# The last pair's second layer as word products instead of products of quarters

## The chip, the cores and the metric

The kernel runs on one core of a Trainium2 chip. The metric is the time of one execution on the device in microseconds (us), the median of several runs. Engines are named as in the profile: PE is TensorE (matrix products, with PEld for its weight loads), DVE is VectorE, ACT is ScalarE, POOL is GpSimd, SP is SyncE, which here only issues transfers. Each engine works through its own instructions strictly in order and waits for others by semaphores.

## The reference

A state-space scan (Mamba-2) over 4 batches, 8 heads and 768 tokens gives a matrix x of 3072 tokens by 256. Then comes a feed-forward block with an ELU between its two layers:

```python
def _moe_ref(x, w_in, w_out):          # x 3072x256, w_in 256x2048, w_out 2048x256
    h = x @ w_in
    alpha = 1.0
    g = np.where(h > 0.0, h, alpha * (np.exp(np.minimum(h, 0.0)) - 1.0))
    return (g @ w_out).astype(np.float32)

x = np.ascontiguousarray(attn_out.transpose(0, 2, 1, 3)).reshape(B * S, H * D)
return _moe_ref(x=x, **moe_kwargs)
```

The change touches `g @ w_out` for the last 512 tokens alone. The weights come to the kernel as 64-bit floats and are turned into float32 in it.

## The kernel before

The 3072 tokens are cut into 12 blocks of 256, numbered 0 to 11 (`n`), and worked on in pairs (n, n + 1). The scan of a later pair is mixed into the feed-forward work of an earlier one. The order of all instructions is written out by hand (a manual schedule): what stands first in the program stands first in the queue of its engine.

**First layer** (`l1_words`, L778, from block 2 on). For each of 16 slices `m` of 128 hidden units it makes h for 512 tokens (two blocks) as three passes over exact 12-bit words. An activation is y1 * 4096 - y0 and a weight is w1 + w0, each word short enough to be exact in TensorE's float32r form; the third pass multiplies sums of words, so that three products do for four. Each pass is two matrix products (L788) of 128x512. The results lie in two PSUM tiles, `ps_h` and `ps_w`. Then:

- ScalarE scales `ps_w` into e (L796), VectorE joins both into `ps_h` (L799);
- `begin_end` (L803): ScalarE's Relu of -h (L805) and Exp (L806) into e;
- `end_words` (L810), called one step later, ahead of the next L799: VectorE's L813 makes g from e and `ps_h` and so frees the PSUM tile. For even m, GpSimd subtracts the first half of g from the second (L817, the helper `sub` of L848), in preparation for the products of quarters.

**Second layer** (`second`, L871). g and w_out of one pair of blocks are taken as 2x2 quarters and multiplied with seven products of quarters instead of eight (Winograd's form). Each of the seven (r = 0 to 6) is made in two halves of the hidden units; one half of one r is four chunks i with two token tiles ts, so eight float32 products of 128x128 (L907), and a pair has 2 x 7 x 8 = 112. The sums of quarters of w_out are made once (`a_out`, `s_out`). The sums of quarters of g are made by GpSimd (`sum_t2`, L863, and the in-place subtractions after r = 0 and r = 1, L922 and L927, all through L848). VectorE and ScalarE add each finished product into `p_sum` and `c_sum` (L885, L919, L944, L959).

**The order.** In the loop of L1310, the first layer of pair n and the second layer of pair n - 2 are interleaved: step k issues `l1_words` for m = k, then some of the scan of a later pair, then `begin_end`, then three or four chunks of `second` (`l2s`). For the last pair (n = 10, where `m` is None) no scan is left; its steps hold only first layer and the second layer of pair 8 (L1330), 56 chunks in all. After it, L1354 runs the second layer of pair 10 by itself. There `last` is set: finished quarters of the output are stored early, and the last product is cut in two (L888 to L899), so that the last store is small.

**PSUM.** Two pools share the eight banks: `ps_a` has seven tiles, which `ps_h`, `ps_w` and every second product of quarters take in turn; `ps_o` has one, which the other products of quarters take.

**SBUF.** Tiles are reused by tag. `w_in` has nine buffers, `w64` eleven, `g0` and `g1` twelve each. At the last pair the `w_in` buffers hold the low words of w_in, and `w64` its high words and the sums of quarters of w_out.

Of the kernel before, what the change touches and what calls it, by code (L numbers as in the profile page):

```python
# [10 lines left out]
F32 = mybir.dt.float32  # L11
U32 = mybir.dt.uint32
BF16 = mybir.dt.bfloat16
F32R = mybir.dt.float32r
ALU = mybir.AluOpType
ACT = mybir.ActivationFunctionType

P = 128
Q = 64
BLK = 2 * P  # L20
CW = 256
WORD = 2.0 ** 12
NEAR = 1.0 + 2.0 ** -13
# [9 lines left out]
def kernel(  # L33
# [27 lines left out]
    nc = tc.nc  # L61
# [3 lines left out]
    NP = NB * NG  # L65
    BH = NB * NH
    ROWS = BH * NG
    DM, DF = moe_w_in.shape
    w_in64, w_out64 = moe_w_in.bitcast(U32), moe_w_out.bitcast(U32)
    KC, MC = DM // P, DF // P  # L70
# [12 lines left out]
    def psum(shape, name):  # L83
        return p_a.tile(shape, F32, tag="a", name=name)
# [7 lines left out]
    for k in range(4):  # L92
        (nc.scalar if k % 2 else nc.sync).dma_start(
            out=la0[BH * k:BH * (k + 1)],
# [715 lines left out]
    def end_words():  # L810
        n, m, h, e = late.pop(0)
        g_of[n, m] = ffn.tile([P, 2, BLK], F32, tag=f"g{m % 2}", name="g", bufs=12)
        nc.vector.scalar_tensor_tensor(  # L813
            out=g_of[n, m].rearrange("p b i -> p (b i)"), in0=e, scalar=1.0, in1=h,
            op0=ALU.subtract, op1=ALU.max)
        if m % 2 == 0 and (n, m) != (2, 14):
            sub(g_of[n, m][:, 1], g_of[n, m][:, 1], g_of[n, m][:, 0])  # L817

    def row_of(n):
        b, g = place(n)  # L820
        return b * S + g * BLK
# [25 lines left out]
    def sub(out, in0, in1):  # L847
        nc.gpsimd.tensor_tensor(out=out, in0=in0, in1=in1, op=ALU.subtract)  # L848

    def quarters(n, i):  # L850


        if n == 2 and i < DIRECT:
            A, B = g_of[n, i], g_of[n + 1, i]
            return A[:, 0], A[:, 1], B[:, 0], B[:, 1]
        A, B = g_of[n, 2 * i], g_of[n, 2 * i + 1]
        return A[:, 0], B[:, 0], A[:, 1], B[:, 1]
# [10 lines left out]

    c_of = {}

    def second(n, last=False):  # L871


        c = c_of[n] = ffn.tile([P, 2, 2, 2, P], F32, tag="c", name="c_sum", bufs=1)
        c11, c12, c21, c22 = (c[:, at, :, e] for e in range(2) for at in range(2))
        a11, a12, s1, a22 = a_out
        s2, s3, s4 = s_out
        for half in range(2):
            if not half:
                tmp = ffn.tile([P, 3, 2, P], F32, tag="tmp", name="p_sum", bufs=1)  # L880
                p1, p5, u = (tmp[:, r] for r in range(3))
            chunk = range(4 * half, 4 * half + 4)

            def add(out, in0, in1, eng=nc.vector):
                eng.tensor_tensor(out=out, in0=in0, in1=in1, op=ALU.add)  # L885

            for r, a in enumerate((a11, a12, s1, s2, s3, a22, s4)):
                if last and half and r == 6:  # L888
                    store(n, 0)
                    for ts, queue in enumerate((nc.scalar, nc.sync)):  # L890
                        ps = psum([P, P], "ps_o")
                        for i in chunk:
                            nc.tensor.matmul(  # L893
                                out=ps, lhsT=quarters(n, i)[3][:, ts * P:(ts + 1) * P],
                                rhs=a[:, i], start=(i == chunk[0]), stop=(i == chunk[-1]))
                        nc.vector.tensor_tensor(
                            out=c12[:, ts], in0=ps, in1=c12[:, ts], op=ALU.add)
                        r0 = row_of(n + 1) + ts * P
                        queue.dma_start(out=out[r0:r0 + P, 0:P], in_=c12[:, ts])  # L899
                    return  # L900
                pool, tag = (p_a, "a") if (7 * half + r) % 2 else (p_o, "o")
                ps = pool.tile([P, 2, P], F32, tag=tag, name="ps_o")
                for i in chunk:
                    b11, b21, b12, b22 = quarters(n, i)
                    b = (b11, b21, b12, t2_of[n, i], b11, b21, b22)[r]
                    for ts in range(2):
                        nc.tensor.matmul(  # L907
                            out=ps[:, ts], lhsT=b[:, ts * P:(ts + 1) * P], rhs=a[:, i],
                            start=(i == chunk[0] and ts == 0), stop=(i == chunk[-1]),
                            skip_group_check=True)  # L910
                    if i < chunk[-1]:
                        yield
                if r == 0:
                    if half:
                        add(p5, ps, c22)
                        add(c21, ps, c21)
                        add(c11, ps, c11)
                    else:
                        nc.scalar.copy(out=p1, in_=ps)  # L919
                    for i in chunk:  # L920
                        b11 = quarters(n, i)[0]
                        sub(b11, t2_of[n, i], b11)  # L922
                elif r == 1:
                    add(c11, ps, c11 if half else p1)
                    for i in chunk:
                        b21 = quarters(n, i)[1]
                        sub(b21, b21, t2_of[n, i])  # L927
                elif r == 2:
                    add(p5, ps, p5 if half else p1)
                elif r == 3:  # L930
                    add(p5, ps, p5)
                    if half:
                        add(c12, c12, p5, nc.gpsimd)
                        add(c21, ps, c21)
                    else:
                        add(u, ps, p1)
                elif r == 4:
                    if half:
                        add(c21, ps, c21)
                    else:  # L940
                        add(u, ps, u)
                    add(c22, ps, p5)
                    if not half:
                        nc.scalar.copy(out=c12, in_=ps)  # L944
                    if last and half:
                        r0 = row_of(n + 1)
                        nc.sync.dma_start(
                            out=out[r0:r0 + BLK, P:2 * P].rearrange("(t p) c -> p t c", p=P),
                            in_=c22)
                    if not half:  # L950
                        sum_t2(n, 1)
                    elif n + 2 < NP:
                        sum_t2(n + 2, 0)
                elif r == 5:
                    add(c21, ps, c21 if half else u)
                elif half:
                    add(c12, ps, c12)
                else:
                    nc.vector.tensor_tensor(out=c12, in0=ps, in1=c12, op=ALU.subtract)  # L959
                yield  # L960

    def store(n, at):
        r0 = row_of(n + at)
        nc.sync.dma_start(
            out=out[r0:r0 + BLK, :].rearrange("(t p) e -> p t e", p=P),
            in_=c_of[n][:, at].rearrange("p t e c -> p t (e c)"))
# [343 lines left out]
    for n in range(4, NP, 2):  # L1310
        m = n + 2 if n + 2 < NP else None
        steps = second(n - 2)

        def l2s(count):
            for _ in range(count):
                next(steps)

        for k in range(16):
            l1_words(n, k, between=m if k == 15 else None)
            turn_step(n, k // 2 * 2 + 1, k % 2)  # L1320
            if n == 4 and k == 0:
                decay(6, 1)
            if m:
                stage_scan(n, k)
            begin_end()
            if k == 0 and n > 4:
                store(n - 4, 0)
                store(n - 4, 1)
            if not m:
                l2s(4 if k % 2 else 3)  # L1330
                continue
            l2s((3 + (n == 4), 3 - (n == 4), 3, 3, 3, 3, 3, 3, 4 + 4 * (n == 4), 5 - 4 * (n == 4),
                 2, 2, 3, 1, 1, 0)[k])
            if k == 9:
                scores(m, m + 1)
                sums(m, m + 1)
                for q in range(4):
                    weigh_two(m, q)
                l2s(2)
                states(m)  # L1340
            if k == 10:
                states(m + 1)
            if k == 13:
                y = across(m, m + 1)
                inside(y, m, m + 1, ts=(0,))
                l2s(4)
                inside(y, m, m + 1, ts=(1,))
        if m:
            l2s(4)
            both_of_y(m)  # L1350
        end_words()
        for _ in steps:
            pass
    n = NP - 2  # L1354
    for k, _ in enumerate(second(n, True)):
        if k == 0:
            store(n - 2, 0)
            store(n - 2, 1)


# [28 lines left out]
```

## Time and profile before

| What | us |
|---|---|
| Median of 3 runs (347.1 to 347.92) | 347.36 |
| The profiled execution, whole | 347.65 |
| Its span in the trace | 345.9 |

Busy time in the span by stretch, us (the first layer of the last pair runs from about 267 to 316, its second layer from 317.65 to 342.7):

| Stretch | PE | DVE | ACT | POOL |
|---|---|---|---|---|
| 0 to 100 | 96.22 | 83.51 | 79.86 | 60.86 |
| 100 to 150 | 49.97 | 41.22 | 41.30 | 45.35 |
| 150 to 210 | 60.00 | 45.00 | 42.73 | 35.77 |
| 210 to 268 | 57.85 | 42.49 | 42.92 | 34.96 |
| 268 to 316 | 48.00 | 31.57 | 28.79 | 23.08 |
| 316 to 346 | 26.67 | 9.48 | 2.47 | 15.23 |

How to read the lines of a profile: a timeline line has the start, the duration, the engine, the line of the program, the operation, the tiles it writes and reads, partitions x elements with the type, and how many instructions were merged into it (x2); in brackets stands how long the engine had been idle before, and what ended that. A line of the chain of work that ended last has the start, the time until the next piece takes over, and the work. Matrix products are pipelined, so a single one is recorded longer than the distance to the next; the distance is what counts. GpSimd's and VectorE's records overlap their neighbours in the same way, by some hundredths of a microsecond. The granted TensorE clock is 0.99 or 1.00 of full speed in each of the stretches above.

### The profile page before, as it was taken

How to read it: one execution, taken by the hardware profiler on the slowest of the kernel's cores; microseconds unless marked ns; L12 is line 12 of the kernel's file. 1: busy time of each engine (PE TensorE's matmuls, PEld its weight loads, DVE VectorE, ACT ScalarE, POOL GpSimd, SP SyncE). 2: the span in 40 equal slices, each digit the busy share in tenths (PEclk: the TensorE clock that was granted, in tenths of full speed). 3: DMA queues.
4: the chain of work that ended last, by engine and by line, in shares of the span. 5: the costliest groups of instructions: out<-in, count | busy, mean ns of one | idle time of the engine just before them, and what ended most of it. 6: DMA issues, size and time to landing. Idle time of an engine off the chain costs nothing.

```text
span 345.9 us, 9861 instructions
## 1 busy us (share of the span) xinstructions
PE 338.7 (98%) x3878; PEld 297.4 (86%) x3878; DVE 253.3 (73%) x504; ACT 238.1 (69%) x541; POOL 215.3 (62%) x321
## 2 busy tenths in 40 slices
PE   8989999999999999999999999999999999999996
PEld 4669888888788898889899888999988999999996
DVE  4898988879898778866788676878676766665222
ACT  5688989599759898657699457699457566565000
POOL 5553553559989699964396664296754264455760
PEclk9999999999999999999999999999999999999999
DMA  8888988470797961070511170410000100001001
GB/s 145 228 231 165 326 178 236 87 140 30 107 151 112 139 108 31 10 162 2 124 45 32 17 153 5 116 22 3 2 0 4 63 0 3 0 0 63 2 1 62
DMA packets 76902, 28.58 MB, mean 83 GB/s; under 512 B 57848, under 2 KB 71736, under 8 KB 76856
## 3 DMA queue, kind: packets, MB, share of 16 engines
q1 hardware_dynamic: 70360, 25.60, 32.2%
q0 software_dynamic: 4176, 2.10, 5.4%
q8 instruction: 30, 0.49, 0.6%
q10 hardware_dynamic: 2320, 0.26, 0.5%
q14 instruction: 16, 0.13, 0.1%
HBM read 22.51 MB, written 3.34 MB: 75 GB/s over the span
## 4 chain that ended last, share of the span: by engine, by line
PE 92%; SPq 2%; DMA 2%; DVE 1%; ACT 1%; issue 1%; POOL 0%; POOLq 0%; ACTq 0%
PE ps_o L907 36%; PE ps_h L788 19%; PE ps_h L671 11%; PE ps_w L788 10%; PE ps_o L832 8%; PE ps_y L638 3%; DMA w<-in_moe_w_in_dram 2%; PE ps_g L545 2%; PE ps_y L620 2%; PE ps_st L575 1%; SPq L179 1%; PE ps_o L893 1%; SPq L132 0%; POOL w_in L252 0%; SPq L116 0%
## 5 line engine op out<-in xcount | busy, mean ns | idle before, releaser
L907 PEld LDWEIGHTS ps_o<-w_out,g 128*128 128x128 f32 x640 | 78.6, 192 | 3.4
L907 PE MATMUL ps_o<-w_out,g 128*128 128x128 f32 x640 | 80.3, 276 | 0.0
L805 ACT ACTIVATE e<-ps_h 128x512 f32<-128x512 f32 x72 | 43.0, 597 | 50.2 <-DVE ps_h L799 50.1
L813 DVE SCALAR_TENSOR_TENSOR g<-e,ps_h 128x512 f32<-128x512 f32 x72 | 49.4, 686 | 34.1 <-ACT e L806 33.7
L848 POOL TENSOR_TENSOR g<-g 128x256 f32<-128x256 f32 x36 | 28.0, 777 | 56.2 <-DVE g L813 56.0
L799 DVE SCALAR_TENSOR_TENSOR ps_h<-ps_h,e 128x512 f32<-128x512 f32 x72 | 50.1, 695 | 12.5 <-ACT e L796 9.7
L788 PE MATMUL ps_w<-y_both,w_words 128*128 128x512 f32 x144 | 51.1, 435 | 0.0
L796 ACT ACTIVATE e<-ps_w 128x512 f32<-128x512 f32 x72 | 42.2, 587 | 12.9 <-PE ps_w L788 12.8
L671 PE MATMUL ps_h<-yT,w_in 128*128 128x256 f32 (+1 forms) x208 | 45.2, 368 | 2.3 <-POOL w_in L252 2.2
L806 ACT ACTIVATE e<-e 128x512 f32<-128x512 f32 x72 | 45.5, 632 | 2.3
L788 PE MATMUL ps_h<-y,w_words 128*128 128x512 f32 x144 | 46.1, 402 | 0.0
L788 PE MATMUL ps_h<-y,w 128*128 128x512 f32 x144 | 44.7, 392 | 0.0
L671 PEld LDWEIGHTS ps_h<-yT,w_in 128*128 128x128 f32 x208 | 36.4, 190 | 8.3 <-POOL w_in L252 3.7
L525 ACT ACTIVATE L<-L,ncum 128x64 f32<-128x64 f32 x160 | 42.2, 336 | 0.2
L907 PE MATMUL ps_o<-w_sum,g 128*128 128x128 f32 x304 | 38.4, 275 | 0.0
L907 PEld LDWEIGHTS ps_o<-w_sum,g 128*128 128x128 f32 x304 | 37.0, 192 | 1.2 <-ACT c_sum L944 0.2
L530 POOL TENSOR_SCALAR_AFFINE_SELECT L<-L 64x512 f32<-64x512 f32 x40 | 30.0, 749 | 9.1 <-ACT L L525 7.7
L788 PEld LDWEIGHTS ps_h<-y,w 128*128 128x128 f32 x144 | 27.1, 188 | 6.5 <-POOL w L848 0.2
L848 POOL TENSOR_TENSOR g<-t,g 128x256 f32<-128x256 f32 x40 | 28.0, 730 | 5.9 <-PE ps_o L907 5.7
L788 PEld LDWEIGHTS ps_h<-y,w_words 128*128 128x128 f32 x144 | 26.4, 188 | 5.7 <-issue 0.4
L832 PE MATMUL ps_o<-w_out,g 128*128 128x256 f32 x128 | 31.0, 384 | 0.0
L848 POOL TENSOR_TENSOR t<-g 128x256 f32<-128x256 f32 x40 | 28.6, 746 | 0.2
(131 smaller groups left out, 535.1 us busy)
## 6 DMA issues: line engine op xcount, KB each, us to landing
L<-flat SPq DMA_DIRECT2D x20, 256.0 KB
w<-in_moe_w_out_dram SPq DMA_DIRECT2D x8, 512.0 KB
w<-in_moe_w_in_dram SPq DMA_DIRECT2D x7, 512.0 KB
xr<-in_x_dram SPq DMA_DIRECT2D x24, 128.0 KB
out_dram<-c_sum SPq DMA_DIRECT2D x9, 256.0 KB
bc<-in_B_dram SPq DMA_DIRECT2D x24, 64.0 KB
w_sum<-w_out POOLq DMA_DIRECT2D x3, 512.0 KB, 8.9
bc<-in_C_dram SPq DMA_DIRECT2D x22, 64.0 KB
```

The source lines that it names most:

```text
L525: nc.scalar.activation(L[:, h, u], L[:, h, u], ACT.Exp, bias=ncum[:, u, row:row + 1])
L530: nc.gpsimd.affine_select(out=part, in_=part, pattern=[[0, 4], [0, 2], [1, Q]], compare_op=ALU.is_ge, fill=0.0, base=0, channel_multiplier=-1)
L671: nc.tensor.matmul(out=ps[:, j, toks], lhsT=w_in[i][:, k, j * P:(j + 1) * P], rhs=yT[n // 2][:, k, n % 2].rearrange("p u i -> p (u i)")[:, ...
L788: nc.tensor.matmul(out=ps, lhsT=lhs[:, k], rhs=rhs[:, k], start=k == 0 and lhs is not w0, stop=k == KC - 1 and lhs is not w1)
L796: nc.scalar.activation(e, both, ACT.Copy, scale=WORD)
L799: nc.vector.scalar_tensor_tensor(out=high, in0=high, scalar=WORD - 1.0, in1=e, op0=ALU.mult, op1=ALU.add)
L805: nc.scalar.activation(e, high, ACT.Relu, scale=-1.0)
L806: nc.scalar.activation(e, e, ACT.Exp, scale=-1.0)
L813: nc.vector.scalar_tensor_tensor(out=g_of[n, m].rearrange("p b i -> p (b i)"), in0=e, scalar=1.0, in1=h, op0=ALU.subtract, op1=ALU.max)
L832: nc.tensor.matmul(out=o_of[n][:, ts], lhsT=g_of[n, j][:, m % 2, ts * P:(ts + 1) * P], rhs=w_out[:, m], start=(m == 0 and ts == 0), stop=( ...
L848: nc.gpsimd.tensor_tensor(out=out, in0=in0, in1=in1, op=ALU.subtract)
L907: nc.tensor.matmul(out=ps[:, ts], lhsT=b[:, ts * P:(ts + 1) * P], rhs=a[:, i], start=(i == chunk[0] and ts == 0), stop=(i == chunk[-1]), s ...
```

## The change

For the last pair, `second` is replaced by `second_words`, and preparations for it are put into the pair's first layer.

- **Words of w_out** (`words_of_out(m)`, 16 calls of one slice each): a scaled high word `v1` on ScalarE, and two instructions on VectorE that make the low word `v0` and the sum `vb`. For even m, GpSimd first puts the slice into a new tile w, half of it copied and half as the difference of two slices (this undoes the sum of quarters that had been added in place into those columns of w_out). Ten of the slices are made in the steps k = 0 to 9 of the pair's first layer, behind that step's chunks of pair 8's second layer, the other six inside `second_words`.
- **Words of g** (`words_of_g(n, m)`, 16 calls of 128x512): the high word `g1` on ScalarE, the sum `gb` on VectorE, the low word `g0` half on GpSimd and half on VectorE. m = 0 and 1 are made in the steps k = 10 and 13, the others in `second_words`, three slices ahead of their products.
- **The products**: for each m and each of four token tiles t three products of 128 tokens x 256 columns in float32r, 16 x 4 x 3 = 192 in all, into four PSUM tiles, one for each t; the last two m are taken tile by tile, so that tile after tile can be evicted (ScalarE, then VectorE) and stored by SP in four stores of 128 KB.
- **Left out for the last pair**: the seven products of quarters with their sums and stores, `sum_t2` for it, and GpSimd's subtraction behind L817. `end_words` for m = 15 moves from the end of the loop into `second_words`, behind the words of g for m = 2 and 3. The stores of pair 8 follow the products of m = 0, as before they followed the first chunk.

The diff, without the parts of `second` that only served `last`:

```diff
--- before.py
+++ after.py
@@ -813,7 +813,7 @@
         nc.vector.scalar_tensor_tensor(
             out=g_of[n, m].rearrange("p b i -> p (b i)"), in0=e, scalar=1.0, in1=h,
             op0=ALU.subtract, op1=ALU.max)
-        if m % 2 == 0 and (n, m) != (2, 14):
+        if m % 2 == 0 and (n, m) != (2, 14) and n + 2 < NP:
             sub(g_of[n, m][:, 1], g_of[n, m][:, 1], g_of[n, m][:, 0])
 
     def row_of(n):
@@ -868,7 +868,7 @@
 
     c_of = {}
 
-    def second(n, last=False):
+    def second(n):
 
 
         c = c_of[n] = ffn.tile([P, 2, 2, 2, P], F32, tag="c", name="c_sum", bufs=1)
@@ -885,19 +885,6 @@
                 eng.tensor_tensor(out=out, in0=in0, in1=in1, op=ALU.add)
 
             for r, a in enumerate((a11, a12, s1, s2, s3, a22, s4)):
...
                 pool, tag = (p_a, "a") if (7 * half + r) % 2 else (p_o, "o")
                 ps = pool.tile([P, 2, P], F32, tag=tag, name="ps_o")
                 for i in chunk:
@@ -942,14 +929,9 @@
                     add(c22, ps, p5)
                     if not half:
                         nc.scalar.copy(out=c12, in_=ps)
...
                     if not half:
                         sum_t2(n, 1)
-                    elif n + 2 < NP:
+                    elif n + 4 < NP:
                         sum_t2(n + 2, 0)
                 elif r == 5:
                     add(c21, ps, c21 if half else u)
@@ -958,6 +940,92 @@
                 else:
                     nc.vector.tensor_tensor(out=c12, in0=ps, in1=c12, op=ALU.subtract)
                 yield
+
+    v_of, h_of = {}, {}
+
+    def words_of_out(m):
+
+        if m < 8:
+            pool, tag, bufs = ((att, "bct", 2), (att, "ctm", None), (raw, "xr", 3), (raw, "bc", 2))[m // 2]
+            v = pool.tile([P, 2, DM], F32R, tag=tag, name="v", **({"bufs": bufs} if bufs else {}))
+            v0 = att.tile([P, DM], F32R, tag="M", name="v0", bufs=8)
+        else:
+            if m % 2 == 0:
+                pair[0] = att.tile([P, 2, 2, DM], F32R, tag="L", name="v", bufs=2) if m == 8 else conv.tile(
+                    [P, 2, 2, DM], F32R, tag="w64", name="v", bufs=W_AHEAD)
+            if m == 12:
+                pair[1] = conv.tile([P, 4, DM], F32R, tag="w64", name="v0", bufs=W_AHEAD)
+            v = pair[0][:, m % 2]
+            v0 = att.tile([P, DM], F32R, tag="ec", name="v0", bufs=4) if m < 12 else pair[1][:, m - 12]
+        w = w_out[:, m]
+        if m % 2 == 0:
+            w = raw.tile([P, DM], F32, tag="b", name="w", bufs=2)
+            nc.gpsimd.tensor_copy(w[:, 0:P], w_out[:, m, 0:P])
+            sub(w[:, P:2 * P], w_out[:, m, P:2 * P], w_out[:, m + 1, P:2 * P])
+        nc.scalar.activation(v[:, 0], w, ACT.Copy, scale=NEAR / WORD)
+        nc.vector.scalar_tensor_tensor(
+            out=v[:, 1], in0=v[:, 0].bitcast(F32), scalar=1.0 - WORD, in1=w,
+            op0=ALU.mult, op1=ALU.add)
+        nc.vector.scalar_tensor_tensor(
+            out=v0, in0=v[:, 0].bitcast(F32), scalar=WORD, in1=w,
+            op0=ALU.mult, op1=ALU.subtract)
+        v_of[m] = v[:, 0], v[:, 1], v0
+
+    pair = [None, None, None]
+
+    def words_of_g(n, m):
+
+        g = g_of[n, m]
+        g1, gb = (conv.tile([P, 2, BLK], F32R, tag="w_in", name="g_words", bufs=DF // CW + 1)
+                  for _ in range(2))
+        nc.scalar.activation(g1, g, ACT.Copy, scale=NEAR)
+        nc.vector.scalar_tensor_tensor(
+            out=gb, in0=g1.bitcast(F32), scalar=1.0 / WORD - 1.0, in1=g,
+            op0=ALU.mult, op1=ALU.add)
+        if m < 2:
+            if m == 0:
+                pair[2] = att.tile([P, 2, 2, BLK], F32R, tag="L", name="g_low", bufs=2)
+            g0 = pair[2][:, m]
+        else:
+            g0 = ffn.tile([P, 2, BLK], F32R, tag=f"g{m % 2}", name="g_low", bufs=12)
+        for b, eng in enumerate((nc.gpsimd, nc.vector)):
+            eng.tensor_tensor(out=g0[:, b], in0=g[:, b], in1=g1[:, b].bitcast(F32), op=ALU.subtract)
+        h_of[m] = [(g1[:, b], gb[:, b], g0[:, b]) for b in range(2)]
+
+    def second_words(n):
+
+        ps = [psum([P, 2, DM], "ps_o") for _ in range(4)]
+
+        def products(m, t):
+            g1, gb, g0 = (w[:, t % 2 * P:(t % 2 + 1) * P] for w in h_of[m][t // 2])
+            v1, vb, v0 = v_of[m]
+            for lhs, rhs, k in ((gb, vb, 1), (g1, v1, 0), (g0, v0, 0)):
+                nc.tensor.matmul(
+                    out=ps[t][:, k], lhsT=lhs, rhs=rhs, start=(m == 0 and k == 1),
+                    stop=(m == MC - 1 and lhs is not g1), skip_group_check=True)
+
+        words_of_g(n, 2)
+        for m in range(MC - 2):
+            if m == 1:
+                end_words()
+            if m + 3 < MC:
+                words_of_g(n, m + 3)
+            if m % 2 == 1 and m < 12:
+                words_of_out(10 + m // 2)
+            for t in range(4):
+                products(m, t)
+            if m == 0:
+                store(n - 2, 0)
+                store(n - 2, 1)
+        for t in range(4):
+            for m in (MC - 2, MC - 1):
+                products(m, t)
+            o = ffn.tile([P, DM], F32, tag="t2", name="o", bufs=4)
+            nc.scalar.activation(o, ps[t][:, 1], ACT.Copy, scale=WORD)
+            nc.vector.scalar_tensor_tensor(
+                out=o, in0=ps[t][:, 0], scalar=WORD - 1.0, in1=o, op0=ALU.mult, op1=ALU.add)
+            r0 = row_of(n + t // 2) + t % 2 * P
+            nc.sync.dma_start(out=out[r0:r0 + P, :], in_=o)
 
     def store(n, at):
         r0 = row_of(n + at)
@@ -1328,6 +1396,10 @@
                 store(n - 4, 1)
             if not m:
                 l2s(4 if k % 2 else 3)
+                if k < 10:
+                    words_of_out(k)
+                if k in (10, 13):
+                    words_of_g(n, k // 3 - 3)
                 continue
             l2s((3 + (n == 4), 3 - (n == 4), 3, 3, 3, 3, 3, 3, 4 + 4 * (n == 4), 5 - 4 * (n == 4),
                  2, 2, 3, 1, 1, 0)[k])
@@ -1348,14 +1420,11 @@
         if m:
             l2s(4)
             both_of_y(m)
-        end_words()
+        if m:
+            end_words()
         for _ in steps:
             pass
-    n = NP - 2
-    for k, _ in enumerate(second(n, True)):
-        if k == 0:
-            store(n - 2, 0)
-            store(n - 2, 1)
+    second_words(NP - 2)
 
 
 # ---- launch: one core; inputs and outputs as the reference has them ----
```

More of the change, by code (lines that the diff above doesn't have):

```diff
@@ L887, in second @@
             for r, a in enumerate((a11, a12, s1, s2, s3, a22, s4)):
[L888 to L900, printed above, removed]
                 pool, tag = (p_a, "a") if (7 * half + r) % 2 else (p_o, "o")
@@ L944, in second @@
                         nc.scalar.copy(out=c12, in_=ps)
[L945 to L949, printed above, removed]
                     if not half:
                         sum_t2(n, 1)
-                    elif n + 2 < NP:
+                    elif n + 4 < NP:
                         sum_t2(n + 2, 0)
```

## The prediction

> **What bounds the kernel now.** I read the page first, then the chain of work that ended last in order of time, then the timeline of each engine over the last pair (267 to 346 us).
>
> ```profile
> span 345.9 us, 9861 instructions
> PE 338.7 (98%) x3878; PEld 297.4 (86%) x3878; DVE 253.3 (73%) x504; ACT 238.1 (69%) x541; POOL 215.3 (62%) x321
> PE 92%; SPq 2%; DMA 2%; DVE 1%; ACT 1%; issue 1%; POOL 0%; POOLq 0%; ACTq 0%
> ```
>
> TensorE is the bound. The chain gives its true pitch (a mean in the groups overlaps its neighbours):
>
> ```profile
> 110.13 3.45 PE ps_o L832 x16
> 300.03 0.46 PE ps_w L788 x2
> 300.50 0.91 PE ps_h L788 x4
> 315.87 25.01 PE ps_o L907 x224
> 340.88 1.80 PE ps_o L893 x16
> ```
>
> A float32 product appears as two records. L907 (128 columns) goes at 25.01/224 = 0.112 us a record. The last 240 records are 16 left of pair 8, up to 315.87 + 16 x 0.112 = 317.65, and pair 10's 224: 25.0 us. A word product (float32r, L788, 512 columns) is one record of 0.228. L832 (float32, 256 columns) takes 0.216 a record.
>
> In pair 10's first layer the other engines go round once per step k, with room to spare:
>
> ```profile
> 280.75 0.69 DVE L799 SCALAR_TENSOR_TENSOR ps_h<-ps_h,e 128x512 f32<-128x512 f32 x1
> 281.48 0.60 ACT L805 ACTIVATE e<-ps_h 128x512 f32<-128x512 f32 x1 [0.88 <-DVE ps_h L799]
> 282.11 0.63 ACT L806 ACTIVATE e<-e 128x512 f32<-128x512 f32 x1
> 282.77 0.69 DVE L813 SCALAR_TENSOR_TENSOR g<-e,ps_h 128x512 f32<-128x512 f32 x1 [0.79 <-ACT e L806]
> 283.88 0.70 DVE L799 SCALAR_TENSOR_TENSOR ps_h<-ps_h,e 128x512 f32<-128x512 f32 x1 [0.42 <-PE ps_h L788]
> 284.72 0.76 DVE L885 TENSOR_TENSOR p_sum<-ps_o,p_sum 128x256 f32<-128x256 f32 x2
> ```
>
> From one L799 to L805 0.73, to L806 0.63, to L813 0.66, to the next L799 0.60 when nothing is awaited: 2.62. TensorE needs (316.54 - 272.71)/15 = 2.92 a step (L799 of steps 0 and 15), so it leads, and VectorE waits 0.42 for it. Two L885 take 0.76, one 0.42: 0.33 each when they follow each other.
>
> Last, what VectorE and GpSimd do to each other:
>
> ```profile
> 117.84 0.68 DVE L738 SCALAR_TENSOR_TENSOR w_words<-w_words,w_in 128x512 fp32r<-128x512 f32 x1
> 117.87 2.46 POOL L848 TENSOR_TENSOR w<-w_in,w_words 128x256 fp32r<-128x256 f32 x2 [0.86 <-issue]
> 119.05 0.68 DVE L465 TENSOR_TENSOR ctm<-bct,hmask 128x512 f32<-128x512 f32 x1
> 302.02 2.80 POOL L848 TENSOR_TENSOR g<-g,t 128x256 f32<-128x256 f32 x4
> 106.52 2.38 DVE L738 SCALAR_TENSOR_TENSOR w_words<-w_words,w_in 128x512 fp32r<-128x512 f32 x1
> 106.53 1.81 POOL L848 TENSOR_TENSOR w<-w_in,w_words 128x256 fp32r<-128x256 f32 x2
> ```
>
> Four GpSimd subtractions take 2.80 (0.70 each) while VectorE reads PSUM with one operand. Two take 2.46 when VectorE runs L738 and L465, whose operands both lie in SBUF: 0.60 + 0.70 + 0.60 + 0.70 = 2.60 against 2.49 from 117.84 to the end. They took turns. VectorE can also be the loser: 2.38 for an instruction of 0.68.
>
> **The change, part by part.**
>
> *Removed:* pair 10's 224 records (25.0 us), its subtractions on GpSimd (eight behind L817, the t2 and in-place ones, 0.70 each) and its sums on VectorE. Only the 25.0 lies on the path.
>
> *TensorE's new work:* 16 m x 4 t x 3 = 192 records of 256 columns. No row has this form. Bounds: 0.112 (128-column float32 pass) and 0.216 (256-column float32 pass). Half of the 512-column word product is 0.114; that row has the same type, so I take 0.114: 21.9 us, or 1.37 per m. Alone this would save 3.1 us.
> The Trainium skill, "TensorE: Matmul & The Clock Gate", section "Back-to-back issue gap", gives N/2.4 + 2.5 ns, an estimated 109 ns at 256 columns and 216 at 512; the trace has 228 at 512, so the measured price stands, and by the page the 192 would take 20.9.
>
> *Words of w_out during the first layer (k = 0 to 9).* In the instruction order ScalarE's word stands behind L806 of its step, and VectorE's two instructions on it stand ahead of that step's L813. So they lie in the loop: 0.73 + 0.63 + 0.54 (L806 to ScalarE's next) + 0.37 (ScalarE 128x256, as L944's copy) + 0.66 (two of 0.33) + 0.60 = 3.53 against TensorE's 2.92. Queued behind: L813, which frees the PSUM tile, and the next L799. The seven PSUM tiles let TensorE lead by some three steps, no more. Ten loops: 35.3. ScalarE's copies of p1 and c12 now stand in the loop, 0.3 each: 0.6. The word of k = 2 waits for GpSimd's w, queued behind eight subtractions (before: until 281.8; plus w, about 282.8; ScalarE is there at 282.1): 0.7. L799 of step 10 comes at 272.71 + 36.6 = 309.3 (before 301.52).
> Steps 10 and 13 hold words of g: 0.73 + 0.63 + 0.54 + 0.60 + 0.60 + 0.33 + 0.60 = 4.03 each; 11, 12 and 14 take 2.62. L799 of step 15: 309.3 + 8.06 + 7.86 = 325.2 (before 316.54).
> Turns with GpSimd add between 0 and, if each of 20 instructions met one, 20 x 0.70 = 14. GpSimd's runs fill about a quarter of these 36 us, and a pair that meets one loses half an operation and a whole one (1.05): 10 x 1/4 x 1.05 = 2.6. L799: 327.8; L806 ends 0.73 + 0.63 + 0.63 later, 329.8; the first words on ScalarE (m = 2, queued behind it) 0.60: 330.4. TensorE has done m = 0 and 1 by then and waits.
>
> *The feed of the second layer.* Per m: VectorE 0.60 + 0.33, GpSimd 0.70, all with both operands in SBUF: in turns 1.63, above TensorE's 1.37. Fourteen m: 22.8. Words of w_out 10 to 15: VectorE 6 x 0.66 = 4.0, GpSimd three copies and subtractions of 128x128 at about 0.48 (L310 482 ns, L252 508 ns): 2.9. Sum 29.7. Lower bound, no blocking: VectorE's own 13.0 + 4.0 + 0.6 (the last L813) = 17.6. The row above kept 2.49 of 2.60, so I take 0.96 x 29.7 = 28.5: the last words at 358.9.
>
> *End.* Tile t = 0 lacks m = 15, t = 1 to 3 lack m = 14 and 15: 21 x 0.114 = 2.4. Then 0.1, ScalarE 0.37, VectorE 0.42: 0.9. Store and finish as before: the last addition ended at 342.99, the span at 345.9:
>
> ```profile
> 342.70 0.29 DVE L896 TENSOR_TENSOR c_sum<-ps_o,c_sum 128x128 f32<-128x128 f32 x1 [0.53 <-PE ps_o L893]
> ```
>
> that is 2.9. Span: 358.9 + 2.4 + 0.9 + 2.9 = 365.1, 19.2 more. The profiled execution took 347.65 (1.75 around the span), 0.29 above the median 347.36. Forecast: 347.36 + 19.2 = 366.6, **366.5 us**.
>
> *Costed at nothing:* pair 8's stores, on SP after m = 0, with over 25 us of products behind them (about 3 us if they came last). The last L813, now queued behind the words of m = 2 and 3 on VectorE: only m = 15 needs it; without that cover 0.6. ScalarE's words, 0.60 per m plus a few 0.37, lie under the 1.63. GpSimd in the first layer loses eight subtractions (5.6) and gains five pairs of 0.96 and two of 0.70 (6.2).
>
> **Rivals.**
>
> 1. *The 256-column product costs 0.216, as L832.* For: the only 256-column rows. Against: they are float32, and the 512-column word product takes 0.228, not 0.43. Then 2.59 per m beats the feed: 14 x 2.59 = 36.3 from 331, plus 3.8: span 371, time 372.5.
> 2. *A GpSimd run holds VectorE to the run's end.* For: at 106.52 an L738 waited 1.7 us, past the ends of two GpSimd instructions. Against: L465 at 119.05 got its turn between two subtractions. Runs of eight (5.6) near k = 1 and k = 9 and of four (2.8) near k = 5: up to 14.0 instead of 2.6, half of it likely, 7: time 371, at most 378. The Trainium skill, "SBUF — State Buffer", section "SBUF: two separate sides", has the port pair held for one instruction at a time; the 1.7 us wait goes beyond that, so the case keeps its chance.
> 3. *No turns at all; the loop alone.* L799 at 325.2, first words complete 2.6 + 0.93 later, 328.7; TensorE 14 x 1.37 = 19.2; 3.8: span 351.7, time 353.2. Against: 2.46 for two subtractions.
> 4. *TensorE stays the bound* (the other side). If PSUM tiles cover the loop, so that a step costs no more than 2.92, and the feed comes in under 1.37 per m, the products run from 317.65: + 21.9 + 3.8 = 343.4, time 344.9. For: VectorE is busy only 73%. Against: that share says nothing of a loop of waits, and 3.53 and 1.63 are both over the points where it turns.
>
> That the words are not used is excluded: the order of instructions shows 192 such products and no others for pair 10.
>
> **How the numbers follow.** Main case 0.63, its own range 361 to 371 (no turns in the first layer and a feed of 27 against turns at twice my estimate). Rival 1: 0.09, 2: 0.12, 3: 0.09, 4: 0.05; a balance near zero 0.02. The range 357 to 375 leaves out rivals 3 and 4, the balance, and the far part of 2: about 0.2. Within 0.2% (0.7 us) is what a measurement of this kernel can't tell from no change. Faster 0.05, same 0.02, slower 0.93.
>
> **What will show it.** L799 to L799 at some 3.5 us for the ten steps with words of w_out, and TensorE idle there. About 2.1 us per m in the second layer, TensorE idle in it, VectorE's 128x512 word and GpSimd's subtraction recorded longer than 0.68 and 0.73. Products at 0.114. I am wrong if TensorE has no gaps after 272, if the loop stays near 2.9, or if VectorE and GpSimd overlap freely in the second layer.

## The result, and the profile after

The changed kernel takes 365.97 us, the median of five runs (365.76 to 366.08); the kernel before took 347.36 beside it. The ratio is 1.0531, with a 95% interval of 1.0511 to 1.0550. The forecast was 366.5 (357 to 375), slower.

The page of the profiled execution of the changed kernel, its span, its engines and its chain of work that ended last:

```profile
span 364.0 us, 9868 instructions
PE 344.5 (95%) x3846; PEld 297.4 (82%) x3846; DVE 283.2 (78%) x552; ACT 252.1 (69%) x575; POOL 217.6 (60%) x320
...
PEclk9999999999999999999999999999999999899999
...
PE 66%; DVE 15%; ACT 8%; issue 4%; SPq 2%; DMA 2%; POOL 2%; DVEq 0%; ACTq 0%; POOLq 0%
```

TensorE held 92% of the chain before and holds 66% now. VectorE went from 1% to 15%, ScalarE from 1% to 8%. The granted clock is full but for one slice near the end.

One round of the first layer's loop, from VectorE's timeline of the changed kernel (L966 and L969 are VectorE's two instructions on a word of w_out):

```profile
285.21 0.69 DVE L799 SCALAR_TENSOR_TENSOR ps_h<-ps_h,e 128x512 f32<-128x512 f32 x1
285.81 0.41 DVE L885 TENSOR_TENSOR p_sum<-ps_o,p_sum 128x256 f32<-128x256 f32 x1
287.53 0.43 DVE L966 SCALAR_TENSOR_TENSOR v<-v,w_out 128x256 fp32r<-128x256 f32 x1 [1.31 <-ACT v L965]
287.87 0.42 DVE L969 SCALAR_TENSOR_TENSOR v<-v,w_out 128x256 fp32r<-128x256 f32 x1
288.21 0.68 DVE L813 SCALAR_TENSOR_TENSOR g<-e,ps_h 128x512 f32<-128x512 f32 x1
288.80 0.69 DVE L799 SCALAR_TENSOR_TENSOR ps_h<-ps_h,e 128x512 f32<-128x512 f32 x1
```

From L799 to L799 are 3.59 us, where the kernel before needed 2.92 on average. In the bracket VectorE waits 1.31 us for ScalarE's word; L813 had waited for L806 before, which ends ahead of that word. Nothing here is short of throughput: the engines wait for each other in a ring.

Behind the first layer, the first words of g and the GpSimd runs beside them, from the same kernel's timeline of VectorE:

```profile
331.53 0.69 DVE L982 SCALAR_TENSOR_TENSOR g_words<-g_words,g 128x512 fp32r<-128x512 f32 x1 [1.52 <-ACT g_words L981]
332.14 0.96 DVE L992 TENSOR_TENSOR g_low<-g,g_words 128x256 fp32r<-128x256 f32 x1
333.02 1.22 DVE L982 SCALAR_TENSOR_TENSOR g_words<-g_words,g 128x512 fp32r<-128x512 f32 x1
334.16 0.95 DVE L992 TENSOR_TENSOR g_low<-g,g_words 128x256 fp32r<-128x256 f32 x1
```

GpSimd's timeline of the same kernel at that time, three of its halves merged into one line:

```profile
331.64 3.20 POOL L992 TENSOR_TENSOR g_low<-g,g_words 128x256 fp32r<-128x256 f32 x3 [6.07 <-ACT g_words L981]
```

An undisturbed L982 is recorded with 0.69 and an L992 with 0.41. Here they take 1.22 and 0.96, about half a microsecond more each, while three GpSimd halves take 3.20 instead of 2.1: both engines are longer than alone.

Busy time by stretch (stretch, its length, then PE, PEld, DVE, ACT and POOL busy with the number of instructions, the granted clock, the DMA share, GB/s):

```profile
268.00:316.00 48.00, 43.56 (x275) 37.88 (x274) 32.88 (x64) 25.12 (x50) 21.54 (x32) 0.96 0.04 12
308.00:312.00 4.00, 3.83 (x14) 3.03 (x12) 3.35 (x9) 2.02 (x4) 0.00 (x0) 0.57 0.00 0
...
331.00:358.00 27.00, 21.10 (x152) 18.82 (x153) 26.16 (x41) 9.77 (x20) 16.81 (x20) 1.00 0.03 10
358.00:364.00 6.00, 2.18 (x19) 1.98 (x17) 1.70 (x4) 1.54 (x4) 0.00 (x0) 0.93 0.26 89
```

In the first layer TensorE, busy all 48 us before, now works 43.56 of them. In the second layer VectorE is busy in 26.16 of 27.00 us and TensorE in 21.10: VectorE, with its waits for GpSimd, feeds it. The second of the four lines is taken up at the end.

### The profile page after: what moved, and what is told of

It is laid out like the page before. It is cut to its first block, busy times and chain, and to the rows that moved or that the text cites. A ratio compares the mean times of both kernels' runs of the same rounds, so it can differ in the third digit from the quotient of the medians.

```text
span 364.0 us, 9868 instructions
## 1 busy us (share of the span) xinstructions
PE 344.5 (95%) x3846; PEld 297.4 (82%) x3846; DVE 283.2 (78%) x552; ACT 252.1 (69%) x575; POOL 217.6 (60%) x320
## 4 chain that ended last, share of the span: by engine, by line
PE 66%; DVE 15%; ACT 8%; issue 4%; SPq 2%; DMA 2%; POOL 2%; DVEq 0%; ACTq 0%; POOLq 0%
PE ps_o L894 21%; PE ps_h L788 15%; PE ps_h L671 8%; PE ps_w L788 8%; PE ps_o L832 6%; PE ps_o L1003 3%; DVE ps_h L799 3%; ACT e L805 3%; ACT e L806 2%; DVE g L813 2%; PE ps_y L638 2%; DVE g_words L982 2%; DVE v L969 2%; DMA w<-in_moe_w_in_dram 2%; DVE g_low L992 2%
## 5 line engine op out<-in xcount | busy, mean ns | idle before, releaser
L813 DVE SCALAR_TENSOR_TENSOR g<-e,ps_h 128x512 f32<-128x512 f32 x72 | 49.2, 683 | 26.7 <-ACT e L806 26.4
L894 PEld LDWEIGHTS ps_o<-w_out,g 128*128 128x128 f32 x512 | 65.1, 193 | 5.5 <-issue 1.2
L894 PE MATMUL ps_o<-w_out,g 128*128 128x128 f32 x512 | 66.9, 278 | 1.4 <-DVE c_sum L885 1.0
L799 DVE SCALAR_TENSOR_TENSOR ps_h<-ps_h,e 128x512 f32<-128x512 f32 x72 | 49.9, 693 | 9.2 <-ACT e L796 6.3
L788 PE MATMUL ps_w<-y_both,w_words 128*128 128x512 f32 x144 | 51.6, 436 | 1.6 <-ACT e L796 1.5
L806 ACT ACTIVATE e<-e 128x512 f32<-128x512 f32 x72 | 45.5, 632 | 2.3
L788 PE MATMUL ps_h<-y,w_words 128*128 128x512 f32 x144 | 46.7, 406 | 0.2 <-DVE g L813 0.2
L788 PE MATMUL ps_h<-y,w 128*128 128x512 f32 x144 | 45.2, 395 | 0.0
L848 POOL TENSOR_TENSOR g<-g 128x256 f32<-128x256 f32 x28 | 22.3, 795 | 35.5 <-DVE g L813 35.3
L894 PE MATMUL ps_o<-w_sum,g 128*128 128x128 f32 x256 | 32.7, 276 | 1.4 <-DVE p_sum L885 1.0
L894 PEld LDWEIGHTS ps_o<-w_sum,g 128*128 128x128 f32 x256 | 31.3, 192 | 3.1 <-POOL t L848 1.2
L788 PEld LDWEIGHTS ps_h<-y,w 128*128 128x128 f32 x144 | 27.3, 190 | 6.8 <-POOL w L848 0.2
L788 PEld LDWEIGHTS ps_h<-y,w_words 128*128 128x128 f32 x144 | 26.4, 189 | 6.3 <-DVE g L813 0.6
L1003 PE MATMUL ps_o<-v,g_words 128*128 128x256 f32 x128 | 25.0, 293 | 6.5 <-DVE g_words L982 5.9
L992 POOL TENSOR_TENSOR g_low<-g,g_words 128x256 fp32r<-128x256 f32 x16 | 16.1, 1027 | 22.4 <-ACT g_words L981 22.4
```

Source lines behind the costliest of these rows:

```text
L788: nc.tensor.matmul(out=ps, lhsT=lhs[:, k], rhs=rhs[:, k], start=k == 0 and lhs is not w0, stop=k == KC - 1 and lhs is not w1)
L799: nc.vector.scalar_tensor_tensor(out=high, in0=high, scalar=WORD - 1.0, in1=e, op0=ALU.mult, op1=ALU.add)
L806: nc.scalar.activation(e, e, ACT.Exp, scale=-1.0)
L813: nc.vector.scalar_tensor_tensor(out=g_of[n, m].rearrange("p b i -> p (b i)"), in0=e, scalar=1.0, in1=h, op0=ALU.subtract, op1=ALU.max)
L894: nc.tensor.matmul(out=ps[:, ts], lhsT=b[:, ts * P:(ts + 1) * P], rhs=a[:, i], start=(i == chunk[0] and ts == 0), stop=(i == chunk[-1]), s ...
L1003: nc.tensor.matmul(out=ps[t][:, k], lhsT=lhs, rhs=rhs, start=(m == 0 and k == 1), stop=(m == MC - 1 and lhs is not g1), skip_group_check=True)
```

## The experiments

Two theories are to be told apart, each with a rival: in the first layer, that the added time comes from *where* the words stand in the ring of waits (rival: from VectorE's added work, or nothing there matters because the feed behind it decides); in the second layer, that VectorE and GpSimd take turns (rival: they don't hinder each other, VectorE's own work or TensorE's products decide). The edits are shown shortened, and some lines are drawn together. The kernel before took between 347.43 and 347.76 beside these runs; each ratio is to the one beside it.

### e1_behind: the words out of the ring

VectorE's two instructions on a word are issued one step later, ahead of an L813 whose word has long been there, and GpSimd's tiles w two steps ahead.

```diff
-                if k < 10:
-                    words_of_out(k)
-                if k in (10, 13):
-                    words_of_g(n, k // 3 - 3)
+                if 0 < k < 11:
+                    out_rest(k - 1)                # VectorE's two
+                if k in (11, 14):
+                    g_rest(n, k // 3 - 3)          # sum and low word
+                if k in (0, 2, 4, 6):
+                    for i in (0, 2) if k == 0 else (k + 2,):
+                        out_w(i)                   # GpSimd's w
+                if k < 10:
+                    out_high(k)                    # ScalarE's word
+                if k in (10, 13):
+                    g_high(n, k // 3 - 3)
```

> The changed kernel with VectorE's instructions on the words of w_out (steps 0 to 9) and of g (steps 10 and 13) issued one step later, behind the L799 of the next step, so that they wait for no instruction of ScalarE's own step; GpSimd's tile w is made two steps ahead. Same work, another order. Theory (a loop of waits made the step 3.53 us and more): the step is TensorE's 2.92 again, L799 of step 15 comes near 317 instead of 328.99, the feed of the second layer stays at some 26 us: 366.0 - 12 = 354 us (353 to 356). Rival (VectorE and ScalarE simply have too much work in the first layer): the order changes little, 364 to 366 us.

Measured: 353.99 us, ratio to the kernel before 1.0185 (1.0159 to 1.0211). Twelve of the 18.6 us go without removing one instruction. The order, not the amount, cost them. Where the first layer then ends is read from e5_both below, which has the same order in it: L799 of step 15 comes at 317.26 instead of 328.99.

### e2_vector_low and e3_no_gpsimd_half: GpSimd out of the second layer's feed

In the first, VectorE makes the whole low word from m = 2 on; in the second, GpSimd's half is left out and that product takes the high word instead.

```diff
# e2_vector_low
+        if m >= 2:
+            nc.vector.tensor_tensor(out=g0, in0=g, in1=g1.bitcast(F32), op=ALU.subtract)
# e3_no_gpsimd_half
         for b, eng in enumerate((nc.gpsimd, nc.vector)):
+            if m > 1 and b == 0:
+                continue
...
+        h_of[m] = [(g1[:, b], gb[:, b], g0[:, b] if b or m < 2 else g1[:, b]) for b in range(2)]
```

> The changed kernel with the low word of g for m = 2 to 15 made wholly by VectorE (one 128x512 subtraction) instead of half by GpSimd and half by VectorE. VectorE's own work grows by 14 x 0.27 = 3.8 us, GpSimd's 14 x 0.70 goes. Theory (the two take turns, so their times add): the feed falls from 26.2 to between 14 x 1.20 + 4.6 = 21.4 and 24.3: 361 to 364 us. Rival (they overlap freely and VectorE's own work is the bound): up to 3.8 us more, 366 to 370 us.

> The changed kernel without GpSimd's half of the low words of g for m = 2 to 15 (the product of the low word takes the high word there instead, so that half of the tokens come out without their low words). VectorE's and TensorE's work are the same. Theory of turns: VectorE's feed falls to its own 17.6 and up to 2.9 of turns with GpSimd's tile w, below TensorE's 14 x 12 x 0.119 = 20.0, which then bounds: 6 us less, 360 us (359 to 361). Rival (no turns): 366 us, unchanged.

Measured: 361.68 us (1.0428; 1.0394 to 1.0462) and 358.56 us (1.0320; 1.0296 to 1.0343); the second lies 0.4 below its expected range. VectorE got more work in e2_vector_low and the kernel became 4.3 us faster. VectorE's timeline there:

```profile
330.88 0.69 DVE L982 SCALAR_TENSOR_TENSOR g_words<-g_words,g 128x512 fp32r<-128x512 f32 x1 [1.52 <-ACT g_words L981]
331.49 0.68 DVE L995 TENSOR_TENSOR g_low<-g,g_words 128x512 fp32r<-128x512 f32 x1
332.09 0.68 DVE L982 SCALAR_TENSOR_TENSOR g_words<-g_words,g 128x512 fp32r<-128x512 f32 x1
332.69 0.68 DVE L995 TENSOR_TENSOR g_low<-g,g_words 128x512 fp32r<-128x512 f32 x1
```

The stretched records are gone: one m takes 1.21 us, a pitch of 0.60 for each instruction. From the first L982 to the last L995's end are 22.7 us, where the changed kernel needed 26.2. The turns are shown. Without the half (e3_no_gpsimd_half) the same stretch takes 19.0, and TensorE is busy 10.00 of 10 us from 340 to 350: it is the bound again.

### e4_before_words and e9_before_behind: the words alone, in the kernel before

The kernel before, its seven products of quarters and all, with the ten words of w_out made and not used: once in the order of the change, once in that of e1_behind.

```diff
                 l2s(4 if k % 2 else 3)
+                if k < 10:
+                    words_of_out(k)      # e9_before_behind: out_rest(k - 1), out_w, out_high(k)
                 continue
```

> The kernel before, with one part of the change alone: the ten words of w_out made in steps 0 to 9 of the last pair's first layer, as the changed kernel makes them, but never used; the second layer of the last pair stays the seven float32 products of quarters. Theory (the loop): TensorE stalls 6 to 8 us in the first layer, 353 to 356 us. Rival (the words fit into the time in which VectorE was idle, 16 of 48 us): 347 to 348 us.

> The kernel before with the ten words of w_out made and not used, as in e4_before_words, but VectorE's two instructions of each one step later and GpSimd's tiles two steps ahead. If the whole 11 us of e4_before_words came from where the words stand in the order of the engines: 347.4 to 348.5 us. If the added work itself costs (VectorE then works 11.2 of 12 us between 292 and 304), 350 or more.

Measured: 358.49 us (1.0335; 1.0305 to 1.0365) and 347.90 us (0.9997; 0.9982 to 1.0011). The same instructions cost 11 us in one order and nothing in the other. With the words behind, TensorE is busy 12.00 of 12 us in every stretch from 268 to 316 although VectorE works 11.73 of 12 us in one of them:

```profile
268.00:280.00 12.00, 12.00 (x87) 10.85 (x86) 9.74 (x18) 6.98 (x15) 7.02 (x11) 1.00 0.14 46
280.00:292.00 12.00, 12.00 (x83) 10.91 (x82) 11.73 (x23) 8.44 (x18) 9.59 (x16) 1.00 0.00 1
```

The expectation for e4_before_words was too low, by 2.5 at its upper end. Its L799 of step 10 comes at 311.89, 10.4 later than in the kernel before. Six of the ten rounds are 3.6 (36 for ten), and four are 4.55 to 4.71, 4.2 more together. In three of the four (steps 1, 5 and 9) VectorE's two instructions on the word stand beside a GpSimd run and are recorded with 0.66 to 0.98 instead of 0.42. The fourth shows the wait that the prediction had put at 0.7 (ScalarE's timeline of e4_before_words, step 2):

```profile
281.35 0.63 ACT L806 ACTIVATE e<-e 128x512 f32<-128x512 f32 x1
282.83 0.42 ACT L983 ACTIVATE v<-w 128x256 fp32r<-128x256 f32 x1 [0.85 <-POOL w L848]
```

### e5_both, e6_products_alone and e7_early: do the parts add up, and how far can it go?

e5_both is e1_behind and e2_vector_low together. e6_products_alone keeps e1_behind's first layer and leaves out all words of g from m = 2 and of w_out from slice 10 on; the words that are there serve for all m. e7_early is e5_both with the words of g for m = 2 made in steps 14 and 15, in buffers of words of w_in that are done with, and those for m = 1 one step earlier than there.

```diff
# e6_products_alone, in products()
+            g1, gb, g0 = ... h_of[m % 2] ...
+            v1, vb, v0 = v_of[m % 10]
# e7_early, against e5_both
+        if m == 2:
+            g1, gb, g0 = k_words[5][0][:, 0], k_words[5][0][:, 1], k_words[6][0][:, 0]
-                if k in (11, 14):
-                    g_rest(n, k // 3 - 3)
+                if k in (11, 13, 15):
+                    g_rest(n, (k - 11) // 2)
...
-                if k in (10, 13):
-                    g_high(n, k // 3 - 3)
+                if k in (10, 12, 14):
+                    g_high(n, k // 2 - 5)
```

> The words of the first layer are issued one step later (as in e1_behind) and the low words of g from m = 2 on are made by VectorE alone (as in e2_vector_low). If the loop of waits and the turns between VectorE and GpSimd are two separate costs, one in the first layer and one behind it, their savings add: 366.0 - 12.0 - 4.3 = 349.7 us (349 to 351), the first layer ends as in the kernel before (L799 of step 15 near 316.5 to 318), and TensorE's products start within 4 us of it. If the two hide each other (the feed is what counts and the first layer's end only moves it), at most one of the savings shows: 353 to 354.

> The words of the first layer are issued one step later; behind it only TensorE works: the words of m = 0 and 1 and of the first ten slices of w_out serve for all m, so the words of g from m = 2 on and of w_out from slice 10 on are not made and most of the sum is left out. The theory (256 columns cost 0.1195 a product, no wait between them): 192 x 0.1195 = 22.9 behind an end of the first layer at 317.7 gives 340.6, with 0.9 and 2.9 a span of 344.4 and a time of 346 us (345 to 347.5), 1 to 2 less than the kernel before. If a product costs 0.216 when nothing waits (rival 1 of the prediction), 41.5 us and 364 to 365.

> As e5_both, and the words of g for m = 2 are made in steps 14 and 15 of the first layer, in buffers of words of w_in that are done with, so that the second layer's TensorE finds three slices ready (36 products, 4.3 us) when the first layer ends. Theory: VectorE then needs 13 x 1.28 + 6 x 0.68 = 20.7 behind the first layer, TensorE 22.9, so TensorE is the bound but for short waits: 1 to 2.5 us less than e5_both, 347 to 349 us, even with the kernel before (347.4). Rival: VectorE's two more words in steps 14 and 15 lengthen the loop again by what they save later: the same as e5_both within 0.5.

Measured: 350.24 us (1.0076; 1.0047 to 1.0105), 346.76 us (0.9970; 0.9953 to 0.9987) and 349.55 us (1.0059; 1.0039 to 1.0080).

e5_both: the savings add, 15.7 of 16.3. L799 of step 15 is at 317.26, where the kernel before has 316.54. e6_products_alone: three products take 0.36, so a 256-column word product costs 0.12, not 0.216, and with nothing to wait for in the second layer the design wins 0.3% (0.1 to 0.5 by the interval).

e7_early missed its expectation: 0.7 us less than e5_both instead of 1 to 2.5, and the two intervals overlap, so even the 0.7 is not certain. VectorE's own work was not stretched, but GpSimd did not get on. GpSimd's timeline of e7_early:

```profile
312.13 0.29 POOL L954 COPY w<-w_out 128x128 f32<-128x128 f32 x1
312.38 0.47 POOL L848 TENSOR_TENSOR w<-w_out 128x128 f32<-128x128 f32 x1
323.71 11.66 POOL L954 COPY w<-w_out 128x128 f32<-128x128 f32 x1 [10.87 <-DVE v L983]
335.34 0.45 POOL L848 TENSOR_TENSOR w<-w_out 128x128 f32<-128x128 f32 x1
```

ScalarE's timeline of the same kernel, its next word behind that copy:

```profile
335.82 0.42 ACT L975 ACTIVATE v<-w 128x256 fp32r<-128x256 f32 x1 [5.85 <-POOL w L848]
```

TensorE's timeline, the two waits in its second layer:

```profile
337.69 0.50 PE L1033 MATMUL ps_o<-v,g_words 128*128 128x256 f32 x2 [0.71 <-DVE g_words L1007]
...
340.77 0.51 PE L1033 MATMUL ps_o<-v,g_words 128*128 128x256 f32 x2 [0.67 <-DVE g_words L1007]
```

A copy of 0.29 us is recorded with 11.66, ScalarE waits 5.85 for it, and TensorE's last eviction begins 2.7 later than in e6_products_alone (343.94 against 341.25). The copy ends when VectorE runs out of work, as VectorE's timeline shows:

```profile
333.94 0.69 DVE L1007 SCALAR_TENSOR_TENSOR g_words<-g_words,g 128x512 fp32r<-128x512 f32 x1
334.54 0.69 DVE L1022 TENSOR_TENSOR g_low<-g,g_words 128x512 fp32r<-128x512 f32 x1
336.27 0.42 DVE L980 SCALAR_TENSOR_TENSOR v<-v,w 128x256 fp32r<-128x256 f32 x1 [1.05 <-ACT v L975]
```

VectorE's instructions followed each other without a pause from 323.50 to 335.2, and none of them was stretched. Then VectorE itself waited 1.05 for the word that hung on the copy, and the last words came late.

### e8_ahead: the words that GpSimd and VectorE can make earlier

As e7_early, with GpSimd's w for slices 10, 12 and 14 and the words of w_out 10 and 11 in the first layer (the edit is against e7_early).

```diff
+                if k == 13:
+                    out_w(14)
-                if k in (0, 2, 4, 6):
+                if k in (0, 2, 4, 6, 8, 10):
                     for i in (0, 2) if k == 0 else (k + 2,):
                         out_w(i)
+                if k in (11, 13):
+                    out_high(10 + k // 13)
+                if k in (12, 14):
+                    out_rest(10 + k // 14)
```

> As e7_early, and GpSimd's tiles w for slices 10, 12 and 14 are made in the first layer, ahead of the stretch in which VectorE runs without a pause, and the words of w_out 10 and 11 there too. Theory: in e7_early GpSimd's copy for slice 14 (0.29 us elsewhere) was recorded with 11.66 us, because VectorE left it no gap, and ScalarE waited 5.85 us for it; without that wait and with 1.4 us less of VectorE's work, TensorE finds all words ready: the span of e6_products_alone, 345.1 to 346, and 346.8 to 347.8 us. Rival: the wait was harmless, because TensorE was the bound at that place anyway: no change from e7_early, 349.5 within 0.4.

Measured: 347.18 us, ratio 0.9983 (0.9970 to 0.9997). From the page of this kernel, its span and its chain:

```profile
span 345.4 us, 9853 instructions
...
PE 90%; SPq 3%; DVE 2%; DMA 2%; ACT 1%; issue 0%; POOL 0%; DVEq 0%
```

Its busy time by stretch, columns as above:

```profile
304.00:316.00 12.00, 12.00 (x83) 10.94 (x82) 11.17 (x24) 8.79 (x17) 2.85 (x5) 1.00 0.01 1
316.00:330.00 14.00, 14.00 (x120) 14.00 (x120) 13.02 (x24) 9.09 (x18) 0.00 (x0) 1.00 0.12 39
```

TensorE is the bound to the end, as in the kernel before, and the span is within 0.3 us of e6_products_alone, where it has nothing to wait for. What the change had cost was waits, all of it: the same products and the same words, in another order and partly on another engine, cost nothing. Against e7_early two things changed at once, GpSimd's copies and 1.4 us of VectorE's work, both moved ahead, so the 2.4 us between the two kernels are not split between them. What is left of the gain is 0.2%, and the upper end of its interval is close to no difference.

## Why the prediction was right

Time and sign were right, and the mechanism of the main case was the one at work. Point by point:

- **The ring in the first layer.** Forecast 3.53 a step, measured 3.59 to 3.61 where no GpSimd run met it. Ten steps took 39.0 (272.84 to 311.88); forecast 36.6 and 2.6 for turns, 39.2. That the sum fits so well is in part luck: 0.07 too little in each of ten rounds was made up by the wait of 0.7 for GpSimd's w at k = 2, which did not occur in this kernel (it did, with 0.85, in e4_before_words). The turns were as large as forecast: the rounds that met GpSimd (4.12, 4.64, 4.14 and 4.27) hold about 2.5 of turns, 1.0 of it in step 2, where VectorE's two instructions took 0.91 and 0.96.
- **Steps 10 and 13.** Forecast 4.03, measured 4.63 each. The term left out was a turn inside the step itself: VectorE's half of the low word stands beside GpSimd's half of the same word.

```profile
314.42 0.69 DVE L982 SCALAR_TENSOR_TENSOR g_words<-g_words,g 128x512 fp32r<-128x512 f32 x1 [1.53 <-ACT g_words L981]
315.03 0.96 DVE L992 TENSOR_TENSOR g_low<-g,g_words 128x256 fp32r<-128x256 f32 x1
```

  Twice 0.6 makes the 1.2 by which L799 of step 15 came later than forecast (328.99 against 327.8).
- **The first words** were done on ScalarE by 331.5 (VectorE's L982 follows at 331.53), forecast 330.4: the same 1.1 to 1.2.
- **The feed.** Forecast 28.5 for VectorE and GpSimd in turns, measured 26.2 on VectorE (331.53 to 357.70). This is the mis-sized term: the factor 0.96 came from one pair of rows. Without the fourteen halves, in e3_no_gpsimd_half, the stretch took 19.0 (with a wait of 1.05 for a GpSimd copy in it), and the prediction's own reckoning without them is 0.96 x (13.0 + 4.0 + 2.9) = 19.1; so the halves cost about 7.2, 0.51 each, where 0.96 x 0.70 = 0.67 had been counted. GpSimd's work overlapped some of VectorE's (L813 reads PSUM with one operand), and from 352.7 on no GpSimd record stands beside VectorE. e2_vector_low shows the size of the turns: the feed is 3.5 us shorter with 14 x (0.60 - 0.33) = 3.8 us more of VectorE's own work.
- **TensorE's products.** Forecast 0.114, measured 0.12 (four tiles' evictions, L1024, follow each other at 0.72 for six products). The price lay near the lower bound, as chosen, and didn't matter: the feed covered it.
- **The end.** The last word ended at 357.70 (forecast 358.9), the span at 364.0 (365.1): 6.3 behind it, forecast 6.2.

The errors were +1.1 up to the first words, -2.3 in the feed and +0.1 in the end: -1.1 in the span. What lies around the span was 365.97 - 364.0 = 2.0 instead of 1.5, so 0.5 is left in the time. That the forecast lay within 0.6 us of the result is luck as far as +1.1 and -2.3 worked against each other; that it was right in its mechanism is not.

Of the rivals, rival 1 (products at 0.216) fell by e6_products_alone. Rival 3 (no turns) fell by e2_vector_low and e3_no_gpsimd_half. Rival 4, TensorE as the bound, is what e8_ahead reaches, but only after the order was changed, at 347.2 and not 344.9; L799 of step 15 stands 0.8 later there (317.38), products at 0.12 cost 192 x 0.006 = 1.2 more, and the remaining tenths were not traced. Rival 2, a run that holds the other engine, did not show in the changed kernel, where the two alternate; it showed the other way round in four experiments, VectorE's run holding GpSimd out. The forecast had not considered that direction.

The forecast had costed at nothing pair 8's stores, the last L813, and ScalarE's words. The last L813 was not free: it stands at 335.04 in VectorE's stretch without a pause, and its 0.60 is part of the 26.2. None of the three shows in the chain of waits from 342 to the end, which goes over VectorE's words, the products and the last eviction; its last links are:

```profile
356.76 0.61 DVE g_words L982
357.37 0.04 issue
357.41 2.78 PE ps_o L1003 x21
360.20 0.02 issue
360.22 0.39 ACT o L1024
```

## What to carry to other kernels

Before work is put into the shadow of a busy engine, look where it stands in the order of the helper engines: an instruction between the last input of a ring and the instruction that closes it lengthens every round, while the same instruction one round later, on data that is already there, is free as long as its engine has time left. Where VectorE and GpSimd both work with two operands in SBUF, expect their times largely to add (here about 0.51 of every 0.70), and don't give GpSimd a short job that a gapless VectorE will itself have to wait for. And work out first what the fastest possible version wins: here 25.0 us of products gave way to 23.0, 0.6% of the time, of which 0.3% was measured with nothing to wait for and 0.2% with all the work done.

## What the runs showed of the hardware that was not expected

**GpSimd kept out for 11.66 us.** In e2_vector_low, e5_both and e7_early one GpSimd copy of 0.29 us is recorded with 11.66 us, in e3_no_gpsimd_half with 9.53, and it ends as VectorE pauses. The Trainium skill, "SBUF — State Buffer", section "SBUF: two separate sides", says that whichever of the two starts first has the shared ports for one whole instruction. The runs agree that it is exclusive, but here GpSimd did not come in between VectorE's instructions, some twenty in a row, though in the changed kernel it did. What tells the two cases apart (the copy, or a VectorE whose inputs are all ready in advance) no run separated.

**The granted clock fell after a gap of 1.5 us.** In the changed kernel TensorE was busy 2.47 of 4 us from 304 to 308, with one gap of 1.53 that ended at 307.51; from 308 to 312 the clock was 0.57 (the window shown above), and L788's products took up to 1.13 a pair in place of 0.63:

```profile
307.51 0.73 PE L788 MATMUL ps_w<-y_both,w_words 128*128 128x512 f32 x2 [1.53 <-ACT e L796]
308.42 1.13 PE L788 MATMUL ps_h<-y,w_words 128*128 128x512 f32 x2 [0.17 <-DVE g L813]
309.34 1.06 PE L788 MATMUL ps_h<-y,w 128*128 128x512 f32 x2
```

The Trainium skill, "TensorE: Matmul & The Clock Gate", section "What's actually happening", has the clock halved after an idle window of about 3.4 us; this trace has no idle stretch that long there, so here a window that was partly busy was enough. The fall, to 0.58 to 0.60 of full speed over 4 us, is there in e2_vector_low, e3_no_gpsimd_half and e4_before_words too, each time behind 4 us in which TensorE was busy 1.44 to 2.47. Gaps of 1.33 and 1.35 in the changed kernel's second layer, where TensorE was busy 21.10 of 27 us, left the clock at 1.00. In the changed kernel the fall cost nothing: the step around it took 3.60 (L799 at 308.28 and 311.88) like the others, because the ring and not TensorE set its length.
